# An mLSTM cell and a mixture-of-depths layer on one core: o loads, gates and stores moved back, the expert layers moved from step 8 to step 9

## The chip, the core and the metric

The kernel runs on one core of a Trainium2 chip. Its engines are TensorE (PE, with its weight loads as PEld), VectorE (DVE), ScalarE (ACT), GpSimd (POOL) and SyncE (SP). Each runs its own instructions in order; they wait for one another by semaphores. DMAs are issued by SP (all loads), by ACT (a few at the start) and by POOL (stores, gathers, scatters), and run on the same 16 DMA engines. The metric is the device time of one execution in microseconds (us).

## What is computed

```python
for t in range(S):                       # B, H, S, D = 4, 8, 768, 40
    m_new = maximum(f_gate[t] + m, i_gate[t])
    f_stab, i_stab = exp(f_gate[t] + m - m_new), exp(i_gate[t] - m_new)
    C = f_stab * C + i_stab * outer(v[t], k[t]);  n = f_stab * n + i_stab * k[t]
    y[t] = sigmoid(o_gate[t]) * (C @ q[t]) / maximum(abs(n . q[t]), 1)
# x = y with heads joined: (4, 768, 320); then for each batch b
scores = x @ w_gate
top = the 128 rows of the batch with the largest scores
out = x;  out[top] = x[top] + sigmoid(scores[top]) * (relu(x[top] @ w1) @ w2)     # 320 -> 1024 -> 320
```

All inputs and the output are float32.

## The kernel before, in words

The sequence is cut into 12 steps (N = 12, lines 675 to 742): step n handles 256 positions of batch n // 3, so a batch takes three steps. A step is written out by hand, and what is said of step n mixes the work of several steps:

- `scores(n)` (L291): k times q on PE into pS; `masked(n)` (L303) on DVE multiplies it by the causal mask into P.
- `turn(n + 1, "kT")` (L223): eight PE transposes of the next step's k into two buffers of the pool ps_t, and two ACT copies out of them; `widen(n + 1)` (L214): an ACT copy that spreads q; `turn(n + 1, "qT")`: the same for q, after widen. Where `turn` gets a count, `fill` (L218) first issues that many 128x128 products on constants whose result nobody reads. The counts for steps 0 to 5 are 0, 2, 6, 2, 2 and 4.
- `update(n + 1)` (L259): PE products of k with weighted v into pU; `states(n + 1)` (L271): DVE adds them up to the running states C. pU has one buffer.
- `weigh(n + 2)` (L239): two POOL multiplies of v by the gate factors, into one of three buffers wv.
- `read(n)` (L310) and `attend(n)` (L327): PE products of q with the states, and of P with wv, into pH (one buffer); `divide(n)` (L336): four DVE instructions that give y.
- `sigmoid(n)` (L247): four ACT instructions on the o gate; `output(n)` (L349): two POOL multiplies of y by it into x; `store(n)` (L357): two POOL DMAs of x to the output; `router(n)` (L364): two DVE reductions of x to its scores.

The scores of a batch are ranked when its three steps are done. `spread` (L397) turns the six score columns to rows on PE, ACT copies them, and `ranks` (L425) counts for each row how many scores are larger: three comparisons on DVE (`greater`) and three signs with sums on ACT (`signs`). `select` (L470) makes a one-hot matrix, `numbers` (L513) turns it into row numbers on PE and DVE, `fetch` (L520) gathers the 128 rows of x back from the output on POOL's DMA queue, and `fetched`, `layer1`, `layer2`, `weighed` and `add` run them through the two layers and add the result to the output by an indirect DMA on POOL.

`layers(n)` (L628) holds the two layers of batches 0 and 1, the ranking of batches 1 and 2 and the gates of three steps, in one long stage that takes the place of the rest of step 8. The layers of batch 2 are in the last step and behind it, with those of batch 3.

What sets the order around the change: the program order of each engine, the loads in `queue` (L624), which SP issues at the head of each step, and the rings of four buffers (NB, NO) for k, q, v and o. `load(n)` issues v (2 DMAs), k (2) and q (1), 320 KB each; `load_o(n)` issues the o gate (2 DMAs, 320 KB). A DMA on SP also waits until the one eight places ahead of it has landed. At the start (lines 100 to 107) the order is load 0, load 1, o0, load 2, o1.

Of the kernel before, what the change touches and what calls it, by code (L numbers as in the profile page):

```python
# [26 lines left out]
def _fast(ctx, tc, q, k, v, i_gate, f_gate, o_gate, w_gate, w1_in, w2_in, out):  # L27
# [76 lines left out]
    wg = const.tile([128, DM], FP, name="wg")  # L104
    load_o(0)
    load(2)
    load_o(1)
# [289 lines left out]
    def spread(b, r0, r1, pool=None, copied=True):  # L397

        x, w = x_t[b % 2], r1 - r0
        if pool is None:  # L400
# [6 lines left out]
        return spread_copy(pB, w) if copied else pB  # L407

# [27 lines left out]
    def ranks_third(b, begin):  # L436

        x, d = x_t[b % 2], dep[b]
        if begin:
            d["cnt"] = mod.tile([128, 2 * NS], FP, name="cnt")  # L440
            for r in range(NS):
                greater(b, d["sb"], x[:, r, DM:DM + 1], d["cnt"][:, r:r + 1])
        for r in (NS,) if begin else range(NS + 1, 2 * NS):
            signs(b, d["sb"], x[:, r, DM:DM + 1], d["cnt"][:, r:r + 1])
        if not begin:
            halved(d)
# [173 lines left out]
    def weights2():  # L620
        for h in range(2):
            SP.dma_start(out=w2[:, 4 * h:4 * h + 4], in_=w2_in[512 * h:512 * h + 512].rearrange("(f p) d -> p f d", p=128))

    queue = {0: (load, 3, load_o, 2), 1: (load, 4, load_o, 3, load, 5, load_o, 4), 2: (load, 6, load_o, 5),  # L624
             4: (load, 7, load, 8, weights1, None, load_o, 6), 5: (load_o, 7, weights2, None, load_o, 8), 6: (load, 9),
             7: (load, 10), 9: (load_o, 9, load_o, 10, load, 11, load_o, 11)}

    def layers(n):  # L628
# [9 lines left out]
        sigmoid(n - 2)  # L638
        output(n - 2)
        store(n - 2)  # L640
# [3 lines left out]
        sigmoid(n - 1)  # L644
        output(n - 1)
        store(n - 1)
        layer2(0)
        router(n - 2)
        router(n - 1)
        fetched(1)  # L650
        weighed(0)
        sigmoid(n)
        output(n)
        store(n)
        valued(1)
        layer1(1, 0)
        router(n)
# [7 lines left out]
        dep[2] = {"sb": spread_copy(pB, 2 * NS)}  # L665
        ranks(2)
# [6 lines left out]
        add(1)  # L673

    for n in range(N):
# [7 lines left out]
        if n == 8:  # L683
# [5 lines left out]
        if n in (3, 6, 11):  # L689
            router(n - 1)  # L690
        if n == 4:
            ranks(0)
            select(0)
        if more:
            turn(n + 1, "kT", (0, 2, 6, 2, 2, 4)[n] if n < 6 else 0)
            widen(n + 1)
        if 0 < n and more:
            update(n + 1)
            if n != 9:
                states(n + 1)  # L700
            if n not in (3, 6, 7, 9):
                router(n - 1)
# [5 lines left out]
        if n == 9:  # L708
            numbers(2, ps_s.tile([128, 2, 512], FP, name="pi", tag="s")[:, 0, 0:3])
            states(n + 1)  # L710
        if n + 2 < N and n != 7:
            weigh(n + 2)
        if n == 6:
            fetch(0)
# [3 lines left out]
        if more:  # L718
            turn(n + 1, "qT")
            if n in (3, 7):  # L720
                dep[n // 4] = {"sb": spread(n // 4, 0, 2 * NS)}
# [398 lines left out]
```

## Time and profile before

| | us |
|---|---|
| median of 3 runs (162.68 to 164.01) | 163.51 |
| the profiled execution, device time | 163.37 |
| its span, first to last instruction | 161.3 |
| PE busy (90%) | 144.5 |
| DVE busy | 95.2 |
| ACT busy | 89.0 |
| POOL busy | 84.5 |
| layers stage, from the first scores of step 8 to those of step 9 (78.24 to 108.84) | 30.60 |

The rows of the profile that follow name the line, the engine, the instruction, out<-in, and how many instructions are merged into the row. In a timeline the first column is the start in the span and the second the duration, both in us; in brackets at the end stands how long the engine was idle before it, and what ended that. SPq, ACTq and POOLq are the sequencers, which issue DMAs. Ends of matmuls are modelled, so rows of PE overlap a little.

### The profile page before, as it was taken

The page shows a single profiled execution, that of the slowest core. Times are in us where ns is not written, and L with a number is a line of the kernel's source. Part 1 is how long each engine was busy: PE and PEld are TensorE (multiplying, and loading weights), DVE is VectorE, ACT ScalarE, POOL GpSimd, SP SyncE. Part 2 cuts the span into 40 slices and gives each one's busy share as a digit, 9 for nine tenths or more (in the row PEclk, how much of TensorE's full clock was granted, in tenths as well). Part 3 has the DMA queues.
Part 4 walks back from the last instruction along what each step waited for, and adds up shares of the span by engine and source line. Part 5 has one row for each costly group of instructions (what it writes and reads, how often), then busy time and mean ns, then how long its engine had stood idle before and what let it go on. Part 6 is the DMA issues. An engine that isn't in the chain of part 4 may idle for free.

```text
span 161.3 us, 6676 instructions
## 1 busy us (share of the span) xinstructions
PE 144.5 (90%) x2864; PEld 125.4 (78%) x2864; DVE 95.2 (59%) x251; ACT 89.0 (55%) x179; POOL 84.5 (52%) x114
## 2 busy tenths in 40 slices
PE   7989899998998998899989989799999999999900
PEld 7779789997987987799878779579888897898500
DVE  6478384656769957594596542197776959411000
ACT  1667396566598747425475675874648669213000
POOL 7137278988575492892004969847480924212020
PEclk9999999999999999999999999999999999999995
DMA  4999899999979989999989999999513210330110
GB/s 88 198 163 196 137 169 205 188 186 205 194 169 227 187 161 208 175 262 296 157 240 232 206 266 172 216 190 184 100 45 87 46 39 4 81 41 0 53 51 2
DMA packets 91880, 24.31 MB, mean 151 GB/s; under 512 B 88097, under 2 KB 90466, under 8 KB 91842
## 3 DMA queue, kind: packets, MB, share of 16 engines
q1 hardware_dynamic: 89920, 18.75, 65.1%
q0 software_dynamic: 1728, 4.92, 11.0%
q8 instruction: 24, 0.39, 1.1%
q10 hardware_dynamic: 194, 0.13, 0.3%
q14 instruction: 14, 0.11, 0.2%
HBM read 19.20 MB, written 4.59 MB: 147 GB/s over the span
## 4 chain that ended last, share of the span: by engine, by line
PE 63%; DMA 14%; ACT 7%; issue 5%; DVE 5%; ACTq 1%; POOL 1%; DVEq 0%; POOLq 0%
PE pt L232 10%; DMA k<-in_k_dram 9%; PE pU L267 9%; PE py L576 8%; PE pH L332 7%; PE pH L322 6%; PE pU L560 6%; PE pS L300 4%; PE ph L560 2%; DMA i_sb<-in_i_gate_dram 2%; PE pU L564 2%; DMA xe<-out_dram,idx 2%; PE pX L498 2%; ACT sgn L423 1%; PE pt L221 1%
## 5 line engine op out<-in xcount | busy, mean ns | idle before, releaser
L244 POOL TENSOR_TENSOR wv<-v,cols 64x656 f32<-64x656 f32 x23 | 30.1, 1312 | 25.0 <-DMA v<-in_v_dram 14.1
L354 POOL TENSOR_TENSOR x<-y,so 128x320 f32<-128x320 f32 x24 | 21.1, 896 | 10.9 <-DVE y L346 4.2
L236 ACT COPY qT<-pt 128x512 f32<-128x512 f32 x24 | 13.8, 635 | 17.2 <-PE pt L232 17.2
L250 ACT ACTIVATE so<-o 64x320 f32<-64x320 f32 x48 | 22.4, 467 | 0.9
L234 ACT COPY kT<-pt 128x512 f32<-128x512 f32 x24 | 13.3, 587 | 15.0 <-PE pt L232 15.0
L369 DVE CUSTOM_DVE_ANT_0 scr<-x,wg 128x320 f32<-128x320 f32 x22 | 13.8, 628 | 8.1 <-POOL x L354 6.5
L576 PE MATMUL py<-w,hT 128*128 128x320 f32 x64 | 18.2, 437 | 0.3 <-ACT qT L236 0.3
L279 DVE TENSOR_TENSOR C<-pU,C 128x164 f32<-128x164 f32 x40 | 13.1, 327 | 7.0 <-PE pU L267 5.9
L267 PE MATMUL pU<-wv,k 128*64 128x82 f32 x384 | 16.5, 237 | 0.7 <-issue 0.7
L267 PEld LDWEIGHTS pU<-wv,k 128*64 128x64 f32 x384 | 14.5, 137 | 2.8 <-issue 2.2
L332 PE MATMUL pH<-wv,P 128*64 128x82 f32 x384 | 16.3, 237 | 0.0
L576 PEld LDWEIGHTS py<-w,hT 128*128 128x128 f32 x64 | 11.8, 190 | 5.1 <-ACT qT L236 0.5
L332 PEld LDWEIGHTS pH<-wv,P 128*64 128x64 f32 x384 | 14.4, 136 | 1.8 <-issue 1.0
L232 PE MATMUL pt<-ident,k 128*128 128x128 f32 x96 | 13.7, 279 | 2.3 <-DMA k<-in_k_dram 2.1
L361 POOL DMA_DIRECT2D out_dram<-x x22 | 13.9, 635 | 3.3 <-POOL x L354 3.3
L418 DVE TENSOR_SCALAR_CACHE_REDUCE cmp<-sb,x 128x768 f32<-128x768 f32 (+2 forms) x14 | 12.0, 857 | 6.0 <-ACT sb L412 5.7
L300 PE MATMUL pS<-qT,kT 40*64 40x64 f32 x768 | 14.8, 221 | 0.8 <-issue 0.5
L306 DVE TENSOR_TENSOR P<-pS,mask 128x1024 f32<-128x1024 f32 x12 | 14.6, 1214 | 0.6 <-PE pS L300 0.6
L523 POOL DMA_INDIRECT xe<-out_dram,idx x4 | 4.3, 1086 | 19.9 <-DVE den L341 13.8
L322 PE MATMUL pH<-C,qT 40*64 40x41 f32 x704 | 14.0, 229 | 0.8 <-issue 0.6
L300 PEld LDWEIGHTS pS<-qT,kT 40*64 40x64 f32 x768 | 12.8, 134 | 2.3 <-issue 0.7
L232 PE MATMUL pt<-ident,qw 128*128 128x128 f32 x96 | 13.1, 279 | 1.4 <-ACT qw L216 1.4
(141 smaller groups left out, 229.6 us busy)
## 6 DMA issues: line engine op xcount, KB each, us to landing
k<-in_k_dram SPq DMA_DIRECT2D x24, 160.0 KB, 5.0
q<-in_q_dram SPq DMA_DIRECT2D x12, 320.0 KB, 5.4
v<-in_v_dram SPq DMA_DIRECT2D x24, 160.0 KB, 4.8
o<-in_o_gate_dram SPq DMA_DIRECT2D x24, 160.0 KB, 5.0
out_dram<-x POOLq DMA_DIRECT2D x22, 160.0 KB, 4.4
w<-in_moe_w_dram SPq DMA_DIRECT2D x2, 640.0 KB, 5.8
w<-in_moe_w_dram SPq DMA_DIRECT2D x2, 512.0 KB, 6.0
out_dram<-x SPq DMA_DIRECT2D x2, 160.0 KB, 2.6
```

The lines of the kernel that those rows point to most:

```text
L232: PE.transpose(pt[:, p, :], src[:, c, 2 * p:2 * p + 2, :].rearrange("s j d -> s (j d)"), ident)
L236: ACT.copy(out=T.rearrange("e p (u t) -> e t p u", t=2)[:, c], in_=pt)
L244: (DVE if n == 0 and r else POOL).tensor_tensor(out=wv_t[n % 3][o, :, :, r], in0=v_t[n % NB][o], op=OP.mult, in1=cols[s][o, 0:2, b * H:b * ...
L250: ACT.activation(out=so_t[n % 3][64 * c:64 * c + 64, r], in_=o_t[n % NO][64 * r:64 * r + 64, c], func=AF.Sigmoid)
L267: PE.matmul(pU[64 * j:64 * j + 64, c, p], k_t[n % NB][:, c, 2 * p + j, :], wv_t[n % 3][:, c, 2 * p + j], start=True, stop=True)
L300: PE.matmul(pS[o, j, c, p, :], kT[e, p, t], qT[e, p, t], start=True, stop=True)
L306: DVE.tensor_tensor(out=P.rearrange(flat), in0=pending[n].pop("pS").rearrange(flat), op=OP.mult, in1=mask.unsqueeze(1).to_broadcast([128, ...
L322: PE.matmul(g["pH"][64 * c:64 * c + 64, NP * j + p, r], g["qT"][e, p, t], state[n, 2 * c + r][e, p, :], start=(c, j) not in g["begun"], st ...
L332: PE.matmul(g["pH"][64 * c:64 * c + 64, NP * j + p], g["P"][:, j, c, p, :], wv_t[n % 3][:, c, 2 * p + j], start=(c, j) not in g["begun"], ...
L354: POOL.tensor_tensor(out=x.rearrange(order, j=2, d=D), in0=pending[n]["y"][:, r].rearrange("s (j p) d -> s j p d", j=2), in1=o.rearrange(o ...
L361: (POOL if n < N - 1 else SP).dma_start(out=out[b, a:a + 128, :].rearrange("(r t) d -> t r d", t=64), in_=x_t[b % 2][64 * c:64 * c + 64, 2 ...
L576: PE.matmul(d["py"], hT_t[:, f, half(b)], w2[:, f, :], start=(f == 0), stop=(f == NF - 1))
```

## The change

1. Loads: at the start load 2 is issued ahead of o0, and o1 moves to step 0. In `queue` each o load moves behind one or more k, q, v loads; load 9 goes from step 6 to step 5, ahead of the weights of the first layer; load 10 stays in step 7, ahead of o8; load 11 goes from step 9 to step 8.
2. Gates: the sigmoids of step n move to a later step (`gated_at`), the multiplies to x too (`made`), and the router (`scored`). Steps 1, 5 and 8 have no sigmoid.
3. Stores: those of steps 0 to 2 are issued together in step 4, those of steps 3 to 5 at the end of step 7.
4. `layers` is called in step 9. The sigmoids, output and store of step 9 are now inside it, behind the copy of batch 2's scores. `add(1)` moves out of it to step 10, where it follows `fetch(2)`; `fetch(2)` itself now stands before the q transposes of step 10, it stood at the end of step 9.
5. No fillers: `turn` is called without a count.
6. Ranking of batch 0: its spread is in step 4 in two halves (four and two columns) through the transposes' pool ps_t (`spread_halves`), with two ACT copies; the comparisons are in steps 5 and 6, the three signs in step 5, the selection and the numbers in step 6, the gather in step 7, there ahead of `weigh(9)`. The spread of batch 1 is in step 8.

```diff
     load(1)
     wg = const.tile([128, DM], FP, name="wg")
+    load(2)
     load_o(0)
-    load(2)
-    load_o(1)
...
+    def spread_halves(b):
+        x = x_t[b % 2]
+        sb = mod.tile([128, 128 * 2 * NS], FP, name=f"sb{2 * NS}", bufs=1)
+        for r0 in (0, 4):
+            w = min(4, 2 * NS - r0)
+            pB = ps_t.tile([128, w, 128], FP, name="pB", tag="t")
+            for r in range(w):
+                PE.transpose(pB[:, r, :], x[:, r0 + r, DM:DM + 1].to_broadcast([128, 128]), ident)
+            ACT.copy(out=sb[:, 128 * r0:128 * (r0 + w)], in_=pB.rearrange("p r t -> p (r t)"))
+        return sb
...
+    def compare(b, r0, r1):
+        x, d = x_t[b % 2], dep[b]
+        if r0 == 0:
             d["cnt"] = mod.tile([128, 2 * NS], FP, name="cnt")
+        for r in range(r0, r1):
+            (greater if r < NS else signs)(b, d["sb"], x[:, r, DM:DM + 1], d["cnt"][:, r:r + 1])
...
-    queue = {0: (load, 3, load_o, 2), 1: (load, 4, load_o, 3, load, 5, load_o, 4), 2: (load, 6, load_o, 5),
-             4: (load, 7, load, 8, weights1, None, load_o, 6), 5: (load_o, 7, weights2, None, load_o, 8), 6: (load, 9),
-             7: (load, 10), 9: (load_o, 9, load_o, 10, load, 11, load_o, 11)}
+    queue = {0: (load, 3, load_o, 1), 1: (load, 4, load_o, 2, load, 5), 2: (load, 6, load_o, 3), 3: (load, 7),
+             4: (load, 8, load_o, 4), 5: (load, 9, load_o, 5, weights1, None, load_o, 6), 6: (weights2, None, load_o, 7),
+             7: (load, 10, load_o, 8), 8: (load_o, 9, load, 11), 10: (load_o, 10, load_o, 11)}
+    gated_at = {0: 0, 2: 1, 3: 2, 4: 3, 6: 4, 7: 5, 10: 10}
+    made = {0: 0, 2: 1, 3: 2, 5: 3, 6: 4, 7: 5, 10: 10}
+    scored = {1: 0, 3: 1, 4: 2, 6: 3, 7: 4, 8: 5, 10: 9}
...
         turn(n + 1, "qT")
         dep[2] = {"sb": spread_copy(pB, 2 * NS)}
+        sigmoid(9)
+        output(9)
+        store(9)
         ranks(2)
...
-        add(1)
...
-        if n == 8:
+        if n == 9:
             layers(n)
...
+        if n == 5:
+            compare(0, 0, 2)
+        if n == 6:
+            compare(0, 2, 3)
+            halved(dep[0])
             select(0)
         if more:
-            turn(n + 1, "kT", (0, 2, 6, 2, 2, 4)[n] if n < 6 else 0)
+            turn(n + 1, "kT")
             widen(n + 1)
+        if n == 5:
+            compare(0, 3, 4)
...
+        if n == 10:
             numbers(2, ps_s.tile([128, 2, 512], FP, name="pi", tag="s")[:, 0, 0:3])
             states(n + 1)
+            fetch(2)
+            add(1)
+        if n == 7:
+            fetch(0)
+        if n < 8:
             weigh(n + 2)
+        if n == 4:
+            for i in range(3):
+                store(i)
...
             turn(n + 1, "qT")
+            if n == 5:
+                compare(0, 4, 6)
+            if n in gated_at:
+                sigmoid(gated_at[n])
+            if n == 6:
+                numbers(0, spare(n + 1)[:, 1, 0:3])
...
         attend(n)
+        if n in (4, 8):
+            dep[n // 8] = {"sb": spread_halves(n // 8)}
         divide(n)
+        if n in made:
+            output(made[n])
+            if n > 8:
+                store(n)
+        if n == 7:
+            for i in range(3, 6):
+                store(i)
```

More of the change, by code (lines that the diff above doesn't have):

```diff
@@ L637, in layers @@
         fetch(1)
[L638 to L640 removed]
+        sigmoid(6)
+        output(6)
+        store(6)
         layer1(0, 4)
```

55 lines of the change are left out of this document (16 added, 39 removed).

## The prediction

> **What bounds the kernel now.** I read the page's first line and the windows of the steps, then PE's timeline for the clean length of a step and its holes, then SP's timeline for the order in which loads are issued, then ACT, DVE and POOL where the change inserts something. First the span, and the stretch of steps 1 to 7 (from the first scores of step 1 to those of step 8; behind the busy times stand PE's granted clock, the DMA engines' share and GB/s):
>
> ```profile
> span 161.3 us, 6676 instructions
> ```
> ```profile
> 20.96:78.24 57.28, 54.54 (x1476) 48.64 (x1474) 38.90 (x100) 36.60 (x68) 38.60 (x55) 1.00 0.98 203
> ```
> ```profile
> 22.26 0.33 PE L300 MATMUL pS<-qT,kT 40*64 40x64 f32 x3 [0.16 <-issue]
> ...
> 65.58 0.63 PE L232 MATMUL pt<-ident,k 128*128 128x128 f32 x4 [0.44 <-DMA k<-in_k_dram]
> ...
> 70.80 1.16 PE L300 MATMUL pS<-qT,kT 40*64 40x64 f32 x64
> 71.89 1.09 PE L232 MATMUL pt<-ident,k 128*128 128x128 f32 x8
> 72.92 1.35 PE L267 MATMUL pU<-wv,k 128*64 128x82 f32 x32
> ...
> 75.28 1.09 PE L232 MATMUL pt<-ident,qw 128*128 128x128 f32 x8
> 76.20 0.82 PE L405 MATMUL pB<-ident,x 128*128 128x128 f32 x6
> 76.95 1.36 PE L332 MATMUL pH<-wv,P 128*64 128x82 f32 x32
> 78.24 1.16 PE L300 MATMUL pS<-qT,kT 40*64 40x64 f32 x64
> ...
> 88.63 4.57 PE L576 MATMUL py<-w,hT 128*128 128x320 f32 x16
> ...
> 115.76 1.15 PE L300 MATMUL pS<-qT,kT 40*64 40x64 f32 x60
> ...
> 123.16 1.16 PE L300 MATMUL pS<-qT,kT 40*64 40x64 f32 x64
> ...
> 127.73 0.32 PE L405 MATMUL pB<-ident,x 128*128 128x128 f32 x1 [0.32 <-DVE x L369]
> ```
> ```profile
> L221 PE MATMUL pt<-hot 128*128 128x128 f32 x32 | 4.9, 291 | 0.0
> ```
>
> PE and the DMA engines are both full in steps 1 to 7: PE is busy for 54.54 of 57.28 us, and the DMA share is 0.98. Step 7 runs without a hole: 78.24 - 70.80 = 7.44 us, of which the spread of one batch's scores is 0.66, so a clean step is 6.78. Inside it kT starts at +1.09, update at +2.12, qT at +4.48, and 2.30 remain from qT to the end. Seven clean steps, two spreads and the numbers of one batch (0.3) are 49.1 us; steps 1 to 7 take 57.28. The 8.2 us between are the fillers (4.9) and holes, most of them waits for k. But the fillers stand just ahead of the k transposes: where k is late, taking them out leaves a wait of the same length. So the gain depends on when loads land.
>
> **The loads.** With engines this full, a load moves by what leaves or enters SP's queue ahead of it.
>
> ```profile
> 10.93 2.48 SPq L75 DMA_DIRECT2D o<-in_o_gate_dram  x2
> ...
> 18.11 1.39 SPq L69 DMA_DIRECT2D q<-in_q_dram  x1
> ...
> 37.23 2.37 SPq L75 DMA_DIRECT2D o<-in_o_gate_dram  x2
> ...
> 41.62 2.33 SPq L65 DMA_DIRECT2D k<-in_k_dram  x2
> ...
> 46.56 1.68 SPq L75 DMA_DIRECT2D o<-in_o_gate_dram  x2
> ...
> 50.12 2.87 SPq L65 DMA_DIRECT2D k<-in_k_dram  x2
> ...
> 54.66 2.44 SPq L75 DMA_DIRECT2D o<-in_o_gate_dram  x2
> ...
> 58.88 3.47 SPq L65 DMA_DIRECT2D k<-in_k_dram  x2
> ...
> 68.59 2.35 SPq L615 DMA_DIRECT2D w<-in_moe_w_dram  x1
> ```
> ```profile
> q0 software_dynamic: 1728, 4.92, 11.0%
> ...
> o<-in_o_gate_dram SPq DMA_DIRECT2D x24, 160.0 KB, 5.0
> ```
>
> An o load holds the queue 2.1 us (mean of 2.37, 1.68 and 2.44). A pair of stores goes out on POOL's queue, but on the same engines: q0's 4.92 MB take 11.0% of 161.3 = 17.7 us, so 0.33 MB take 1.2. Ends: 0, if stores fit into gaps, and 2.1, an o load's price for the same bytes; I take 1.2, which is measured on that queue. A load's second half is issued about 1.2 us behind its first (half of 2.4) and lands 5.0 later.
>
> k first. Load 5 now has one o load and two pairs fewer ahead: 41.62 - 2.37 - 2.4 = 36.9, landed by 43.1. Load 6 has two and three pairs fewer: 50.12 - 4.05 - 3.6 = 42.5, landed by 49.7. Load 7: 58.88 - 4.05 - 1.2 = 53.6 (four pairs go, three return in step 4), landed by 59.9. All three are on time for the steps below, so PE's waits for k go.
>
> Now o, which is moved back. o0 goes behind load 2: 18.11 + 1.39 - 2.48 = 17.0, landed 23.2. o3 was ahead of load 5 and is now behind load 6, where o5 was, less o3, o4 and four pairs: 54.66 - 4.05 - 4.8 = 45.8, landed 52.0. o4 follows load 8, where the weights were, less two o loads and two pairs: 68.59 - 4.1 - 2.4 = 62.1, landed 68.3. o5 follows o4 and a load (37.23 + 2.37 to 46.56 is 6.96, less a pair 5.8): 70.0, landed 76.2.
>
> **The change, part by part.** The gates' sigmoids stay in ACT's in-order queue behind the qT copies, and what follows them there waits when o is late: the kT copies and the widening of q, for which PE's qT waits, and in step 4 the two copies of the spread scores, which free both buffers that the k transposes need.
>
> ```profile
> 23.78 1.07 ACT L234 COPY kT<-pt 128x512 f32<-128x512 f32 x2
> 24.88 0.72 ACT L216 COPY qw<-q 128x640 f32<-128x640 f32 x1
> ...
> 45.20 1.95 ACT L250 ACTIVATE so<-o 64x320 f32<-64x320 f32 x4
> ...
> 99.37 0.60 ACT L566 ACTIVATE hT<-ph 128x512 f32<-128x512 f32 x1 [1.90 <-PE ph L564]
> ```
>
> Of POOL I need the multiplies, the gather of batch 2 with what stands behind it, the add of batch 1, and how long a gather takes to land:
>
> ```profile
> 108.98 1.90 POOL L589 DMA_INDIRECT out_dram<-yg,idx  x1 [0.59 <-POOL wv L244]
> ...
> 116.42 1.09 POOL L523 DMA_INDIRECT xe<-out_dram,idx  x1 [0.27 <-DVE den L341]
> 117.93 1.69 POOL L354 TENSOR_TENSOR x<-y,so 128x320 f32<-128x320 f32 x2 [0.42 <-DVE y L346]
> ```
> ```profile
> DMA to landing us min/median/max: 3.1/3.2/6.6
> ```
> ```profile
> L244 POOL TENSOR_TENSOR wv<-v,cols 64x656 f32<-64x656 f32 x23 | 30.1, 1312 | 25.0 <-DMA v<-in_v_dram 14.1 <-DVE cols L206 6.0 <-DMA out_dram<-yg,idx 4.2
> ```
>
> - Step 1: scores end at 22.26 + 0.33 = 22.6 as now, qT could start at 26.0. o0 lands at 23.2, three of four sigmoids (0.49 each) remain, then 1.07 and 0.72: 26.5. Cost 0.5. Steps 2 and 3 are clean: they end at 35.6 and 42.4.
> - Step 4: clean to 49.2, spread to 49.8, scores of step 5 to 50.9. o3 lands at 52.0; three sigmoids to 53.5, the first copy of the spread (0.5, the size of a kT copy) to 54.0. Only then may k be transposed. **Cost 3.1**, the largest new wait.
> - Step 7: o4 at 68.3, three sigmoids, 1.07 and 0.72 end at 71.6; qT's slot is 71.2 (step 5 ends 59.7, step 6 66.7). Cost 0.35.
> - Step 8: the first gather is now issued ahead of weigh(9), whose second half waits for its landing. Output(4) on POOL ends near 71.2, behind o4's gates (69.8) and two multiplies, the first begun before them. From issue to landing 3.2 (median) to 6.6 (longest); I take the middle, 4.9, as the queue is full there. With 1.3 for the second half: 77.4 against an update slot of 75.9. Cost 1.5 (ends 0 and 3.2). The wait for o5's gates (0.9) lies within it.
>
> - Stores later: six at once in steps 4 and 7, on a POOL that waits for v there anyway; their DMA time is in the sums above. No cost beside.
> - Ranking in steps 4 to 7: the same instructions, six transposes and two copies instead of one. Three signs go to step 5, which has no gate, so ACT has room: nothing. It also takes away step 4's wait for q behind three signs, counted in the 8.2.
> - Weights come with o5 ahead of them and load 9: w2's second half lands near 90 by the same count and is asked for at 88.63 + 4.5 = 93.1, as the layers now start at 82.7 (step 7 ends 73.8; 6.78, 0.66 and 1.5 follow). Nothing. o8 lands near 101, one to two us behind its slot in the layers; ACT is idle for 1.90 right behind it (99.37), so I take 0.3 (ends 0 and 2.5).
> - Layers in step 9: the same work, but the gates of step 9 now stand between the copy of batch 2's scores and its three signs.
>
> ```profile
> 107.19 0.19 ACT L423 ACTIVATION_READ_ACCUMULATOR sgn<-sb,x 128x1 f32 x1
> 108.44 0.96 DVE L472 TENSOR_TENSOR sel<-iota,cnt 128x768 bf16<-128x768 f32 x1
> 109.67 1.05 DVE L279 TENSOR_TENSOR C<-pU,C 128x164 f32<-128x164 f32 x3
> 110.95 1.35 PE L267 MATMUL pU<-wv,k 128*64 128x82 f32 x32
> ```
>
> The signs end at 107.4, then the selection (109.4), then the states, which release pU at 110.7; PE writes pU at 110.95. There is 0.2 of slack. 1.95 more on ACT delays this chain: cost 1.8.
>
> - Step 10: add(1) is put behind the gather of batch 2 on POOL and must wait for its landing, as both touch the output. Behind it stands output(10), then the last scores, then the spread for which PE waits already (127.73).
>
> The gather can go about 2 us earlier than now, lands 3.2 later, and 1.9 follow: 5.1 from its issue, where 1.5 lie between gather and output now. 5.1 - 2.0 - 1.5 = 1.6 late, less the 0.3 that PE waits already: cost 1.3 (ends 0 and 3.3).
>
> **The sum.** From 8.2 I take off the hole of 0.5 in step 1's scores, which stays: -7.7. A plain step 8 (6.78) takes the place of step 10 (123.16 - 115.76 = 7.40): -0.6. Costs: 0.5 + 3.1 + 0.35 + 1.5 + 0.3 + 1.8 + 1.3 = 8.9. Span 161.3 - 8.3 + 8.9 = 161.9. The profiled execution took 163.37, so 2.1 lie around the span: 164.0, against its own 163.37 and the median of 163.51.
>
> **Rivals.**
> Faster: the queue drains quicker and o3 is there when ACT asks. If stores cost 2.1 a pair, o3 lands 3.6 earlier, at 48.4, and the 3.1 of step 4 go; with the later gates on time too, 0.9 more: 164.0 - 4.0 = 160.0. It decides from a landing by 48.9. For it: queues held by buffer releases are gone. Against: k4 to k6 now come at a steady pace under a share of 0.98.
>
> Slower: PE stands idle for 3.1 us before step 5's k. The granted clock is 1.00 in every stretch quoted, but the longest hole there is under 0.7. If the clock halves behind a hole of this length, the rest of that step (5.7) doubles at worst: 164.0 + 5.7; I take half, 166.9. It decides where the hole outlasts the clock's patience. [...]
>
> Slower as well: the gather lands at 6.6 and POOL's chain in step 10 costs its upper end: 164.0 + 1.7 + 2.0 = 167.7.
>
> No effect: PE already hides everything, so that only waits change names. That is nearly the forecast; it says 163.4.
>
> **How the numbers follow.** Forecast, with the second no-effect case, 0.50, by itself 162 to 166; faster rival, whole or in part, 0.29; the two slower ones 0.21. The range reaches to 160.0 and to 168.0. 1% (1.6 us) is about what can be told from no change. Above 165.1 lie the slower rivals and a third of the forecast: 0.38; below 161.9 the faster one: 0.30; between 0.32.
>
> **What would show it.** Right: no waits for k in steps 2 to 6; ACT's gates of step 4 waiting for o until about 52; PE idle about 3 us ahead of the k transposes of step 5; layers starting near 82.7; PE's update in step 10 waiting for DVE; add(1) waiting for the gather. Wrong: o3 landed before 49, a granted clock under 1.00 in steps 5 or 6, or a wait for weights.

## The result, and the profile after

The changed kernel takes 175.86 us (median of 4 runs, 174.80 to 176.88) where the kernel before takes 163.76 (4 runs on the same chip, 162.68 to 164.12): ratio 1.075, 95% interval 1.067 to 1.083. It is slower, by more than the range forecast. The profiled execution took 176.88 us with a span of 175.0. Single executions of one kernel differ by some us, the longer ones mostly at a lower mean clock (beside experiment 4 the kernel before took 163.34 at 0.987 and 173.22 at 0.954), and the ratios compare undisturbed executions alone.

Windows by stage, first one of before, then four of after (from, to and length; then the busy times of PE, PEld, DVE, ACT and POOL; PE's granted clock; DMA share; GB/s):

```profile
123.16:161.30 38.14, 29.42 (x347) 24.92 (x344) 15.09 (x44) 13.62 (x36) 10.34 (x11) 0.95 0.15 34
```
```profile
51.41:64.33 12.92, 8.84 (x210) 7.88 (x209) 5.99 (x12) 7.19 (x14) 7.51 (x10) 0.74 1.06 219
...
88.47:123.74 35.27, 31.15 (x339) 25.58 (x338) 16.49 (x40) 21.87 (x48) 18.15 (x21) 0.90 0.89 178
123.74:132.09 8.35, 7.00 (x217) 6.32 (x214) 6.67 (x19) 4.06 (x10) 3.82 (x3) 1.00 0.14 31
132.09:175.00 42.91, 31.03 (x347) 26.23 (x344) 13.62 (x44) 13.62 (x36) 12.79 (x13) 0.90 0.18 38
```

With the other windows of both kernels that gives this table (us). The forecast's column is its own timetable: step 5 begins at 50.9 - 1.1, ends at 59.7, the layers begin at 82.7, and step 10 is the old step 9 (6.92) with the cost of 1.8 (rounded, the column adds up to 161.7, its sum is 161.9).

| stage | before | after | difference | forecast |
|---|---|---|---|---|
| up to the scores of step 5 | 54.51 | 51.41 | -3.1 | 49.8 |
| step 5 | 8.19 | 12.92 | +4.7 | 9.9 |
| the other plain steps up to 10 (before 6, 7, 9, 10; after 6, 7, 8, 10) | 29.86 | 32.49 | +2.6 | 31.7 |
| layers | 30.60 | 35.27 | +4.7 | 30.9 |
| last stage, from the scores of step 11 | 38.14 | 42.91 | +4.8 | 39.4 |

The gain came: before step 5 the kernel is 3.1 us ahead, and no step waits for k any more (in the page of after the group of the k transposes, L231, is idle for 4.1 us in all, and ACT ends all of it). Then the other four rows give back 16.8. PE's timeline shows most of it, each wait in brackets:

```profile
56.65 1.97 PE L231 MATMUL pt<-ident,k 128*128 128x128 f32 x8 [4.08 <-ACT sb L419]
58.55 2.46 PE L266 MATMUL pU<-wv,k 128*64 128x82 f32 x32
```
```profile
92.22 0.58 PE L299 MATMUL pS<-qT,kT 40*64 40x64 f32 x9 [2.70 <-issue]
...
93.56 1.93 PE L321 MATMUL pH<-C,qT 40*64 40x41 f32 x48
95.42 2.45 PE L331 MATMUL pH<-wv,P 128*64 128x82 f32 x32
```
```profile
127.28 1.35 PE L266 MATMUL pU<-wv,k 128*64 128x82 f32 x32 [1.35 <-DVE C L278]
...
139.63 0.48 PE L406 MATMUL pB<-ident,x 128*128 128x128 f32 x1 [3.41 <-DVE x L368]
...
140.54 3.09 PE L569 MATMUL pU<-xeT,w 128*128 128x128 f32 x16
```

Waits are only half of it. Behind the long ones the same rows take up to twice as long: the eight transposes 1.97 (1.09 elsewhere), the update 2.46 (1.35), attend 2.45 (1.36), layer 1 3.09. The clock itself shows why. These are windows of after of 3.41 us each, set on the times at which the granted clock changes:

```profile
50.75:54.17 3.42, 1.82 (x70) 1.36 (x67) 2.92 (x7) 0.47 (x1) 3.42 (x6) 1.00 1.02 220
54.17:57.58 3.41, 0.93 (x5) 0.93 (x6) 0.67 (x1) 2.26 (x5) 0.31 (x1) 0.50 1.06 286
57.58:60.99 3.41, 3.41 (x41) 2.90 (x39) 1.37 (x4) 2.83 (x5) 1.93 (x2) 0.50 0.89 180
60.99:64.33 3.34, 3.34 (x107) 3.03 (x105) 1.64 (x5) 1.63 (x3) 2.50 (x3) 1.00 1.26 183
```
```profile
91.71:95.13 3.42, 2.91 (x58) 2.41 (x60) 2.26 (x4) 1.42 (x4) 0.00 (x0) 0.50 0.76 154
95.13:98.54 3.41, 3.41 (x43) 3.15 (x40) 2.76 (x6) 2.45 (x6) 0.00 (x0) 0.50 1.06 162
```
```profile
139.50:142.91 3.41, 3.11 (x14) 2.82 (x15) 1.61 (x6) 0.59 (x1) 3.29 (x4) 0.50 0.42 96
```

In this trace the granted clock is either 1.00 or 0.50, and the times at which it changes lie whole multiples of 3.41 us apart: it falls at 54.17, 91.71 and 139.50 (11 and 14 times 3.41 apart), for two, two and one windows, and then not before PE's last product. In the window ahead of the first fall PE stood for 1.60 us (3.42 - 1.82); in the next, at half clock, for 2.48, and the one behind that was at half too. PE was busy for 4.34, 6.32 and 3.11 us at half clock in these three places (0.93 + 3.41, 2.91 + 3.41, 3.11); half of that, 6.9 us in all, is an estimate of what a whole clock would have saved (the slow rows less their lengths elsewhere give 6.2).

What made PE wait shows on the other engines. ACT in step 4, then POOL in steps 10 and 11:

```profile
52.77 0.47 ACT L249 ACTIVATE so<-o 64x320 f32<-64x320 f32 x1 [2.75 <-DMA o<-in_o_gate_dram]
54.54 1.45 ACT L249 ACTIVATE so<-o 64x320 f32<-64x320 f32 x3 [1.30 <-DMA o<-in_o_gate_dram]
56.01 0.86 ACT L419 COPY sb<-pB 128x512 f32<-128x512 f32 x2
```
```profile
131.41 1.11 POOL L532 DMA_INDIRECT xe<-out_dram,idx  x1 [4.46 <-PE pt L231]
135.82 1.66 POOL L598 DMA_INDIRECT out_dram<-yg,idx  x1 [3.30 <-ACT so L249]
137.55 1.67 POOL L353 TENSOR_TENSOR x<-y,so 128x320 f32<-128x320 f32 x2
```

ACT's gates of step 4 wait for both halves of o3; the copies of the spread scores come last and PE's transposes wait for them. On POOL the add waits from 132.5 until behind the landing of the gather (135.02 by the trace; the name in the bracket, ACT, had long been done), and output(10) starts at 137.55.

The hole of 2.70 (a stretch in which PE stands) is put down to "issue": PE waited for nothing that a semaphore shows. The trace has 24 packets of 16 KB of kind instruction (queue q8, 0.39 MB), and each of the seven holes of PE over 0.2 us that are put down to issue in the steps ends 1.4 to 1.8 us behind the end of such a packet, here at 90.75. These holes also stand 256 PE instructions or a multiple of that apart (with 449, 705, 1473, 3265, 3521, 3777 and 4033 of them ahead; in before the three holes stand at 449, 3777 and 4801). From that comes the estimate that a packet brings 256 instructions (the trace has 5742 of PE's, 239 for each of the 24), and that PE had run out of them. Call each such place in PE's instructions a mark. The packet that ended the long hole took 0.96 us, as others do, but it started late: 5.0 us behind PE's passing of the mark before (84.78), where the four packets ahead of it started 1.6 to 2.1 us behind theirs. The 16 DMA engines, of whose time these packets take 1.0% over the span, also carried this:

```profile
w<-in_moe_w_dram SPq DMA_DIRECT2D x2, 640.0 KB, 9.1
```

The two halves of weights 2 took 8.6 and 9.5 us from issue to landing, against 5 for a load of k, q or v, and the half of an o load issued right behind them 9.3; six stores went out beside them (81.6 to 85.2).

### The profile page after: what moved, and what is told of

It reads as the page before. It is cut to its first block, busy times and chain, and to the rows that moved or that the text cites. A ratio compares the mean times of both kernels' runs of the same rounds, so it can differ in the third digit from the quotient of the medians.

```text
span 175.0 us, 6617 instructions
## 1 busy us (share of the span) xinstructions
PE 148.0 (85%) x2832; PEld 128.4 (73%) x2832; DVE 95.4 (55%) x251; ACT 88.9 (51%) x181; POOL 85.6 (49%) x114
## 4 chain that ended last, share of the span: by engine, by line
PE 48%; SPq 11%; issue 10%; DMA 9%; ACT 9%; DVE 5%; POOL 3%; POOLq 0%; DVEq 0%; ACTq 0%
PE pt L231 8%; SPq L65 7%; PE pH L331 7%; PE pU L569 6%; DMA o<-in_o_gate_dram 6%; PE py L585 5%; PE pU L266 4%; PE pH L321 4%; PE pS L299 4%; DMA xe<-out_dram,idx 4%; PE ph L569 2%; ACT so L249 2%; PE pU L573 2%; ACT kT L233 2%; SPq L75 2%
## 5 line engine op out<-in xcount | busy, mean ns | idle before, releaser
L243 POOL TENSOR_TENSOR wv<-v,cols 64x656 f32<-64x656 f32 x23 | 31.3, 1363 | 24.8 <-DMA v<-in_v_dram 11.8
L266 PE MATMUL pU<-wv,k 128*64 128x82 f32 x384 | 17.9, 247 | 2.1 <-DVE C L278 1.3
L299 PE MATMUL pS<-qT,kT 40*64 40x64 f32 x768 | 15.3, 223 | 4.9 <-issue 4.6
L266 PEld LDWEIGHTS pU<-wv,k 128*64 128x64 f32 x384 | 15.6, 144 | 4.6 <-issue 3.0
L331 PE MATMUL pH<-wv,P 128*64 128x82 f32 x384 | 17.4, 246 | 0.0
L231 PE MATMUL pt<-ident,k 128*128 128x128 f32 x96 | 13.9, 291 | 4.1 <-ACT sb L419 4.1
L278 DVE TENSOR_TENSOR C<-pU,C 128x164 f32<-128x164 f32 x40 | 13.1, 328 | 7.2 <-PE pU L266 6.1
L331 PEld LDWEIGHTS pH<-wv,P 128*64 128x64 f32 x384 | 15.4, 144 | 1.7 <-issue 1.2
L321 PE MATMUL pH<-C,qT 40*64 40x41 f32 x704 | 14.8, 235 | 0.5 <-issue 0.5
L321 PEld LDWEIGHTS pH<-C,qT 40*64 40x64 f32 x704 | 13.3, 140 | 2.2 <-issue 1.3
L231 PEld LDWEIGHTS pt<-ident,k 128*128 128x128 f32 x96 | 11.1, 148 | 5.0 <-ACT sb L419 4.2
```

What stands on the lines that cost most here:

```text
L231: PE.transpose(pt[:, p, :], src[:, c, 2 * p:2 * p + 2, :].rearrange("s j d -> s (j d)"), ident)
L243: (DVE if n == 0 and r else POOL).tensor_tensor(out=wv_t[n % 3][o, :, :, r], in0=v_t[n % NB][o], op=OP.mult, in1=cols[s][o, 0:2, b * H:b * ...
L266: PE.matmul(pU[64 * j:64 * j + 64, c, p], k_t[n % NB][:, c, 2 * p + j, :], wv_t[n % 3][:, c, 2 * p + j], start=True, stop=True)
L299: PE.matmul(pS[o, j, c, p, :], kT[e, p, t], qT[e, p, t], start=True, stop=True)
L321: PE.matmul(g["pH"][64 * c:64 * c + 64, NP * j + p, r], g["qT"][e, p, t], state[n, 2 * c + r][e, p, :], start=(c, j) not in g["begun"], st ...
L331: PE.matmul(g["pH"][64 * c:64 * c + 64, NP * j + p], g["P"][:, j, c, p, :], wv_t[n % 3][:, c, 2 * p + j], start=(c, j) not in g["begun"], ...
```

## The experiments

The theory: four waits (o3 late; PE's instructions late behind weights 2 and the stores; the add behind the gather; gates ahead of the signs). The first three cost PE over 1.6 us each, with half clock behind, the fourth 1.35 at whole clock. The main rival: the slow rows come from something else, such as the missing fillers. In the edits `...` stands for lines left out, and of `queue` only the entries that change are shown.

**1. o3 ahead of load 6.**

```diff
-2: (load, 6, load_o, 3)
+2: (load_o, 3, load, 6)
```

> The changed kernel (175.9) with o3 issued ahead of load 6 instead of behind it. Theory (o3 lands too late, the gates of step 4 block ACT ahead of the copies of the spread scores, and the wait of 4.08 also drops the clock): o3 is issued some 10 us earlier, PE's wait before the k transposes of step 5 falls from 4.08 to under 0.5, kT returns from 1.97 to 1.09 and the update of that step from 2.46 to 1.35, step 5 takes about 7.0 instead of 12.92: some 5.6 us, so about 170.3. Rival 1 (the load is only exchanged for another: k of step 6 or 7 comes late by the 2.1 us of an o load): the wait moves to step 6 or 7 and the time is 172 to 174. Rival 2 (the rows of step 5 are slow for want of the fillers, not for the wait): the wait goes, the slow rows stay: about 172.3.

Measured: 170.14 (169.5 to 170.8), 1.035 times before (1.027 to 1.044); after stands at 1.075.

```profile
51.66:59.43 7.77, 7.30 (x210) 6.31 (x209) 5.34 (x11) 5.62 (x11) 7.57 (x10) 1.00 1.01 204
59.43:68.82 9.39, 7.38 (x200) 6.57 (x198) 7.37 (x15) 4.29 (x9) 4.94 (x5) 1.00 0.88 195
68.82:79.35 10.53, 8.72 (x212) 7.71 (x209) 6.13 (x20) 5.33 (x10) 4.75 (x5) 0.84 1.06 194
...
87.39:117.28 29.89, 28.18 (x339) 23.03 (x339) 16.82 (x40) 21.86 (x48) 18.10 (x21) 1.00 1.04 224
```

Step 5 falls from 12.92 to 7.77 at whole clock: the wait and the slow rows went together. The total is as expected (5.7), but not by this alone. The layers fell by 5.4, because the instructions came in time there (no hole, though weights 2 still took 8.6 us to land, 9.1 in after), and steps 6 and 7 grew by 1.7 and 3.2: a new hole of 1.75 for instructions behind the six stores, and, as the steps now come earlier, the same wait for the next gate (o4, PE idle for 1.77, with a half clock behind it: 0.84 over step 7).

**2. Fillers in two waits of the changed kernel.**

```diff
         if n == 5:
+            fill(spare(n + 1)[:, 0, :], 13)
             compare(0, 0, 2)
...
             fetched(b - 1, 2)
+            fill(ps_t.tile([128, 128], FP, name="pf", tag="t"), 10)
```

> The changed kernel with 13 filler products ahead of the k transposes of step 5 (13 x 0.29 = 3.8 us in a wait of 4.08) and 10 ahead of the spread of step 11 (2.9 us in a wait of 3.41). Nothing is ready earlier by it. Theory (an idle PE of 3 to 4 us loses granted clock, and the rows behind run slow): the waits are filled, the rows behind return to 1.09 (kT of step 6), 1.35 (update) and 1.95 (layer 1 in the last stage, now 3.09); 2.0 and 1.1 to 1.4 us less, so 172.5 to 172.9. Rival (the slow rows come from the DMA load or the kind of work there, or the stages are bound by another engine): rows stay slow, or are fast with no gain, time 175.9; if the fillers outlast the waits, up to 176.5.

Measured: 169.38 (166.7 to 171.8; too far apart for an interval), the profiled one 166.67.

```profile
51.77 3.17 PE L220 MATMUL pU<-hot 128*128 128x128 f32 x26
54.77 1.04 PE L231 MATMUL pt<-ident,k 128*128 128x128 f32 x8
55.74 1.35 PE L266 MATMUL pU<-wv,k 128*64 128x82 f32 x32
...
130.44 0.32 PE L406 MATMUL pB<-ident,x 128*128 128x128 f32 x1 [0.69 <-DVE x L368]
...
131.25 1.95 PE L569 MATMUL pU<-xeT,w 128*128 128x128 f32 x16
```

(Each product is two records.) Products that compute nothing make the kernel faster: transposes 1.04, update 1.35, layer 1 1.95, all at whole clock, step 5 9.73 and the last stage 41.50. These rows are the clock by itself, 2.0 us in step 5 and 1.5 in the last stage. The other 1.2 us of step 5 are not: o3 landed at 52.41 in this execution (54.52 in after), so the wait was shorter too. Nor are the further 3.7 us in the layers (31.56) the edit's: a hole of 1.77 for instructions came there too, but lay across two of the windows of 3.41 us, 0.49 and 1.28 us, and the clock stayed at 1.00. That such holes fall differently from run to run fits the spread, but only one of the four runs has a trace.

**3. Stores 3 to 5 spread over steps 5 to 7.**

```diff
             output(made[n])
-            if n > 8:
-                store(n)
-        if n == 7:
-            for i in range(3, 6):
-                store(i)
+            if made[n] > 2:
+                store(made[n])
```

> The changed kernel with the stores of steps 3, 4 and 5 right behind their outputs (in steps 5, 6 and 7) instead of all six at the end of step 7. Theory (six stores and the two halves of weights 2 crowd the DMA engines between 82 and 92 us, PE's next 16 KB of instructions come late, PE stands for 2.70 inside the scores of step 9 and loses clock): the landing times of the halves fall from 8.6 and 9.5 towards 6, the hole falls under 1.0, layer 1 and the rows before it return to full clock, layers 35.3 to about 31 us: about 171.4. Rival (the hole comes from the place in PE's code or from weights 2 alone): a hole of 2 us or more stays, time 175.9. Second rival: the stores taken earlier delay loads 9 and o5 and give back up to 1.2 a pair: 173.

Measured: 175.76 (174.3 to 177.9), 1.060 (1.048 to 1.073). A miss: weights 2 land in 6.9, but PE still waits 1.88 at the same place (PE row below), and the clock falls behind it (0.95 over the layers). The hole is not made by these stores alone; it is 0.8 shorter in this execution.

```profile
90.65 0.38 PE L299 MATMUL pS<-qT,kT 40*64 40x64 f32 x9 [1.88 <-issue]
```

**4. Weights 2 behind load 10 and o8.**

```diff
-6: (weights2, None, load_o, 7), 7: (load, 10, load_o, 8),
+6: (load_o, 7), 7: (load, 10, load_o, 8, weights2, None),
```

> The changed kernel with the two halves of weights 2 behind load 10 and o8 in SP's queue, some 6 us later, so that they are issued in the layers' stage, where PE uses few instructions per us. The stores stay bunched. Theory (each half is 0.66 MB that SP hands over faster than the engines move it; the queues get 8 to 9 us deep in step 8, a plain step that uses up instructions quickly, and PE's next 16 KB come late): the hole of 2.70 in the scores of step 9 falls under 0.6, the half clock behind it (6.8 us, of which 6.3 busy) goes; 2.2 + 3.1 less, so about 170.5. Rival 1 (the hole belongs to its place in PE's code or to the stores): it stays near 2, time 175 to 176. Rival 2 (weights 2 then lands too late for layer 2 of batch 0): the hole goes and PE waits there for w2 by 1 to 2 us: 172 to 173.

Measured: 174.33 (173.8 to 176.0), 1.063 (1.051 to 1.076).

```profile
92.89:122.78 29.89, 28.18 (x339) 23.03 (x338) 16.82 (x40) 21.86 (x48) 18.10 (x21) 1.00 0.84 181
```
```profile
53.41:56.82 3.41, 0.00 (x0) 0.00 (x0) 0.78 (x1) 1.97 (x5) 1.40 (x3) 1.00 1.05 273
56.82:60.23 3.41, 2.87 (x22) 2.54 (x24) 2.04 (x4) 2.19 (x5) 1.41 (x2) 0.50 1.03 207
60.23:63.65 3.42, 3.42 (x87) 3.17 (x86) 1.64 (x5) 1.41 (x3) 2.85 (x3) 0.50 1.11 190
63.65:67.06 3.41, 3.41 (x32) 3.08 (x34) 0.00 (x0) 2.15 (x4) 0.00 (x0) 0.50 0.90 169
```

The hole of the layers is gone, and they take 29.89 instead of 35.27: the expected 5.3. Two other places took most of it back in this execution. In step 8, where other loads now stand, a hole of 1.63 came. And the wait of step 5, untouched by the edit and 4.47 long here, filled one window of 3.41 us whole; the clock then stayed at half for three windows, the last two of them fully busy, and step 5 took 15.75.

**5. The add of batch 1 back at the end of the layers.**

```diff
     def layers(n):
...
         states(n + 1)
+        add(1)
...
             fetch(2)
-            add(1)
```

> The changed kernel with the add of batch 1 back at the end of the layers' stage. Theory (the add behind the gather of batch 2 waits for its landing and holds output(10), and the 3.41 that PE then waits in step 11 also costs clock): PE's wait ahead of the spread in step 11 falls from 3.41 to about 0.3, layer 1 behind it from 3.09 to about 1.95; 3.1 + 1.2 less: about 171.5. Rival 1 (the clock there is not tied to the wait): only the wait goes, 172.8. Rival 2 (the gather of batch 2 then stands behind the add and lands as late, so another engine ends as late): over 174.5.

Measured: 171.13 (164.75, 170.5, 171.8 and 172.2), the profile taken at 172.23.

```profile
132.35:170.50 38.15, 29.50 (x346) 24.92 (x344) 13.55 (x44) 13.61 (x36) 11.82 (x12) 0.96 0.17 38
```
```profile
136.90 0.32 PE L406 MATMUL pB<-ident,x 128*128 128x128 f32 x1 [0.22 <-DVE x L368]
137.06 1.95 PE L569 MATMUL pU<-xeT,w 128*128 128x128 f32 x16
```

The last stage is back at before's 38.14; the edit is worth 4.76 there (3.4 of wait, 1.1 in layer 1). The total fits the 171.5 expected as far as runs this far apart can tell; the profiled execution is 4.65 under that of after.

**6. The gates of step 9 behind the signs of batch 2.**

```diff
-        sigmoid(9)
-        output(9)
-        store(9)
         ranks(2)
+        sigmoid(9)
+        output(9)
+        store(9)
```

> The changed kernel with the gates, output and store of step 9 behind the signs of batch 2. Theory (the gates hold the signs, the signs hold the selection, the selection holds the states that free pU): the wait of 1.35 ahead of the update in step 10 falls to about 0.1; step 10 takes 7.0 instead of 8.35. The time of one run can not tell 1.35. Rival (output(9) comes later by it and delays something behind it on POOL): the wait goes, the last stage grows by as much.

Measured: one run, 179.4. DVE in after, then DVE, PE and POOL here:

```profile
124.12 0.69 DVE L446 TENSOR_SCALAR cnt<-cnt 128x3 f32<-128x3 f32 x1 [1.86 <-ACT sgn L436]
```
```profile
122.35 0.17 DVE L446 TENSOR_SCALAR cnt<-cnt 128x3 f32<-128x3 f32 x1
```
```profile
129.56 2.45 PE L266 MATMUL pU<-wv,k 128*64 128x82 f32 x32 [3.59 <-POOL wv L243]
```
```profile
123.26 1.83 POOL L353 TENSOR_TENSOR x<-y,so 128x320 f32<-128x320 f32 x2 [4.14 <-ACT so L249]
...
126.68 2.83 POOL L243 TENSOR_TENSOR wv<-v,cols 64x656 f32<-64x656 f32 x2
```

DVE's wait for the signs went (1.86 before), which shows the mechanism. But output(9) now waits for its gates on POOL ahead of the weighing of step 11, and PE's update waits 3.59 for that, more than twice what was mended, with half clock behind it. Step 10 takes 14.49 at a mean clock of 0.68. The rival had the engine right and the place wrong.

**7. The kernel before without its fillers.**

```diff
-            turn(n + 1, "kT", (0, 2, 6, 2, 2, 4)[n] if n < 6 else 0)
+            turn(n + 1, "kT")
```

> The kernel before, with its 16 filler products of steps 0 to 5 taken out and nothing else. Theory (the fillers fill waits for k; taken out without the moved loads, most of their 4.9 us turn into waits of the same length, each under the 1.6 us of idle in a window of 3.4 us that cost clock so far): span within 2 us of before, 161.5 to 164, granted clock as before. Rival 1 (the fillers hold the clock up): a half clock of 3.4 us or more in steps 3 to 6, 165 to 168. Rival 2 (the fillers are pure cost): 4 to 5 us less, about 159.

Measured: 168.25 (165.1 to 170.9), 1.009 (0.991 to 1.028), no difference that can be told.

```profile
20.92:77.78 56.86, 51.18 (x1444) 45.08 (x1442) 41.86 (x101) 36.69 (x68) 38.64 (x55) 1.00 1.00 206
81.47:84.88 3.41, 1.72 (x38) 1.46 (x34) 3.09 (x8) 2.95 (x6) 0.00 (x0) 1.00 0.95 319
84.88:88.30 3.42, 3.42 (x18) 3.20 (x17) 0.80 (x1) 0.00 (x0) 0.00 (x0) 0.50 1.08 203
```

Steps 1 to 7 take 56.86, with the fillers 57.28. PE is busy for 3.4 us less (51.18 instead of 54.54), and 2.9 of that has become idle time (5.7 now, 2.7 before; the holes now are 1.77, 0.61 and 0.28 for k, 1.23 for q's widening, 1.48 for DVE), at whole clock. So the fillers neither cost nor hold up anything in the steps: the rival that their absence slows the rows fails. The span is 164.3 because of a hole for instructions, now in the layers: PE idle for 1.69 of one window, half clock in the next.

**8. All four places mended, first version.** The edits of 1, 4, 5 and 6 together, and o4 ahead of load 8.

```diff
-4: (load, 8, load_o, 4),
+4: (load_o, 4, load, 8),
```

> The changed kernel with five places mended: o3 ahead of load 6 and o4 ahead of load 8, weights 2 behind o8, the add of batch 1 back at the end of the layers, the gates of step 9 behind the signs of batch 2. Theory (the costs are those waits and the clock lost behind them, and they add up): steps 5 to 7 about 7.7 each, layers about 30, step 10 about 7.0, the last stage 38.1 as before: span 158, time about 160, under the kernel before. Rival (each mended wait uncovers the next of its size, for k of step 8 or for weights 2): 163 to 167.

Measured: 176.29 (173.8 to 178.6), 1.069 (1.051 to 1.086), a clear miss.

```profile
102.26 2.47 PE L585 MATMUL py<-w,hT 128*128 128x320 f32 x4 [7.03 <-DMA w<-in_moe_w_dram]
```

Steps 5 to 7 came near the 7.7 forecast (7.88, 8.85, 7.93). But the layers now begin 3 us earlier than in the changed kernel and 7 earlier than in 4, and weights 2, moved back, are too late for them (7.03, and three windows of half clock, 0.50 from 97.25 to 107.49), and the weighing of step 11 waits as in 6 (3.60). Mends that work alone need not add up.

**9. Second version.** As 8, but weights 2 where the change has them, the weighing of step 9 ahead of the first gather, that of step 11 ahead of output(9).

```diff
         sigmoid(9)
-        output(9)
-        store(9)
         layer2(1)
...
         weigh(n + 2)
+        output(9)
+        store(9)
...
-        if n == 7:
-            fetch(0)
         if n < 8:
             weigh(n + 2)
+        if n == 7:
+            fetch(0)
```

> The changed kernel with o3 ahead of load 6, o4 ahead of load 8, the add of batch 1 back at the end of the layers, the gates of step 9 behind the signs of batch 2 and the weigh of step 11 ahead of output(9), the weigh of step 9 ahead of the first gather; weights 2 where the change has them. Theory (the costs are single waits with the half clock behind them; the two that the last version uncovered, on weights 2 and on the weigh of step 11, were made by its own moves): steps 5 to 7 take 7.9, 8.8 and 7.9 as there, step 8 about 8.2, layers 29.9, step 10 about 7.0, the last stage 38.1: span 159, time about 161, 1.5% under the kernel before. Rival 1 (another hole of over 1.6 us in one window appears, in step 8 or in the layers, for PE's instructions or for weights 2, with 3.4 to 6.8 us at half clock behind it): 164 to 167. Rival 2 (what each mend gains, the next queue gives back): 170 and more.

Measured: 168.27 (167.4 to 170.9), 1.029 (1.015 to 1.042).

```profile
61.04 0.57 PE L299 MATMUL pS<-qT,kT 40*64 40x64 f32 x21 [1.48 <-issue]
...
77.59 0.93 PE L299 MATMUL pS<-qT,kT 40*64 40x64 f32 x48 [1.38 <-issue]
```

Rival 1: layers 29.89 and step 10 6.93 as hoped, but two holes for instructions, in steps 6 and 8, each with about one window of half clock (mean clock 0.83 and 0.84), make them 10.25 and 10.74. And as output(9) now stood ahead of the add of batch 1, the gather waited for the add; the last stage was 43.2.

**10. Third version.** As 9, and the stores one pair a step, the add ahead of output(9), router(9) behind the numbers of batch 2.

```diff
-    scored = {1: 0, 3: 1, 4: 2, 6: 3, 7: 4, 8: 5, 10: 9}
+    scored = {1: 0, 3: 1, 4: 2, 6: 3, 7: 4, 8: 5}
...
+        add(1)
         output(9)
...
         states(n + 1)
-        add(1)
...
             states(n + 1)
+            router(9)
             fetch(2)
...
-        if n == 4:
-            for i in range(3):
-                store(i)
...
-        if n == 7:
-            for i in range(3, 6):
-                store(i)
+        if 3 <= n <= 8:
+            store(n - 3)
```

> The last version with three more places mended: the stores of steps 0 to 5 one pair a step (3 to 8) instead of two groups of six; the add of batch 1 ahead of output(9); router(9) behind the numbers of batch 2 and ahead of the gather, so that the gather is issued near where the kernel before has it. Theory (six stores at once hold up PE's next 16 KB of instructions, 1.48 and 1.38 us in steps 6 and 8, each with 3.4 us at half clock behind; in step 11 the gather waited 4.79 for an add that stood behind output(9)): steps 6 and 8 take about 7.3 each instead of 10.25 and 10.73, the last stage 38.1 instead of 43.2: span 155 to 156, time about 157.5, 4% under the kernel before. Rival 1 (the late instructions come from the sum of the DMA load, not from the stores being bunched): one of the two holes stays, with its half clock: 161 to 163, the kernel before's time. Rival 2 (stores in steps 3 to 8 delay k of steps 6 to 8 by 1.2 a pair): waits for k of 1 to 2 us, 160 to 164.

Measured: 162.61 (12 runs, 161.0 to 164.7) beside 163.15, ratio 0.997 (0.993 to 1.001): the kernel before's time, which is rival 1's figure, and not the 157.5 of the theory. The granted clock is 1.00 in each stage from step 5 to step 10, and 0.93 in the last (0.95 in before).

```profile
54.25 0.63 PE L231 MATMUL pt<-ident,k 128*128 128x128 f32 x4 [1.55 <-DMA k<-in_k_dram]
...
76.50 0.93 PE L299 MATMUL pS<-qT,kT 40*64 40x64 f32 x48 [1.11 <-issue]
```

The hole of step 6 is gone and the last stage takes 38.5; a wait for k in step 5 and 1.11 and 0.74 of late instructions in step 8 are left. Rivals 1 and 2 hold in part each.

**11. The same with the stores in two groups again.**

```diff
+        if n == 4:
+            for i in range(3):
+                store(i)
...
-        if 3 <= n <= 8:
-            store(n - 3)
+        if n == 7:
+            for i in range(3, 6):
+                store(i)
```

> The last version with one thing put back: the stores of steps 0 to 5 in two groups of six, as the change has them. Theory (six stores at once hold up PE's next instructions in steps 6 and 8): holes of 1.2 us or more, put down to issue, come back in the scores of steps 6 and 8 (1.48 and 1.38 in the version before), with a half clock of 3.4 us behind at least one; the wait for k of 1.55 in step 5 goes; together +1.5 to +4 us, 164 to 166.6. Rival (which hole comes is a matter of the moment, and the stores have no part in it): 161 to 163, holes like those of the last version (1.11 and 0.74 in step 8, none in step 6).

Measured: 164.62 (164.3 to 166.1), 1.010 (1.002 to 1.019).

```profile
60.55 0.57 PE L299 MATMUL pS<-qT,kT 40*64 40x64 f32 x21 [1.21 <-issue]
...
81.88 1.97 PE L231 MATMUL pt<-ident,qw 128*128 128x128 f32 x8 [2.62 <-ACT qw L215]
```

The hole of step 6 is back and the wait for k gone: six stores at once do hold up PE's instructions there (holes of 1.75, 1.20, 1.48 and 1.21 in the versions of 1, 8, 9 and 11, none in the two with spread stores). In step 8 no hole for instructions came; instead ACT waited for o5, the widening of q stood behind the gates, and PE waited 2.62 with half clock behind (0.74 over the step). So the theory holds for step 6 and not for step 8.

**12. The third version with the stores a step later.**

```diff
-        if 3 <= n <= 8:
-            store(n - 3)
+        if 4 <= n <= 8:
+            store(n - 4)
+        if n == 8:
+            store(5)
```

> The last version with the spread stores one step later (step 4 to 8, two pairs in step 8), so that two pairs fewer stand ahead of k of step 6. Theory (the 1.55 that PE waits for k in step 5 are one to two pairs of stores at 1.2 us each): that wait falls to 0.5 or less, nothing else changes: about 161.5, 1% under the kernel before. Rival (the second pair in step 8 makes the holes there, 1.11 and 0.74 now, larger, past the idle time that costs the clock): 163 to 165.

Measured: 163.92 (12 runs, 161.6 to 165.9) beside 163.64, ratio 0.998 (0.993 to 1.003). Step 5 takes 6.96, without the wait for k, but PE waits 1.11 for k in step 7 and 2.65 in step 8 for the same gate (o5) as in 11, and the time is that of 10. No version beats the kernel before by more than can be measured.

## Why the prediction was wrong

The mechanisms were mostly right, their order of size was not, and two terms were missing. The gap of 13.1 us of span (175.0 against 161.9), step by step:

- **The loads: right.** No wait for k is left in steps 2 to 6. The gain came out 1.6 smaller by step 5 (51.41 against 49.8), 0.4 in step 1, 0.85 in step 3 (a hole for instructions of 0.65 in it) and 0.35 in step 4, which the clean step did not allow for.
- **Step 4, "cost 3.1, the largest new wait": right in cause, near in size.** o3 landed at 54.52 instead of 52.0, the wait was 4.08. The faster rival, which needed it by 48.9, fell with that.
- **The slower rival, the clock: it was the case, and in three places instead of one.** The prediction put 2.9 on step 5 and made it hang on the length of one hole. Measured by the estimate above: 2.2 in step 5, 3.2 in the layers, 1.6 in step 11, 6.9 in all (6.2 by the rows), about half of the gap. This is the main step that failed: the sum put the clock at nothing, and no run shows that a hole of 3.1 us is free of it, or that the length of one hole decides. What the runs show is idle time by window of 3.41 us. Whole-clock windows followed by half clock had 1.60, 2.20 and 3.28 us of it in after, 1.69 in experiment 7 and all 3.41 in experiment 4. Those with the most that were followed by whole clock had 1.53 and 1.10 in before and 1.35 in after. A hole of 1.77 that two windows shared (0.49 and 1.28, experiment 2) cost no clock.

  A count of work fits these two traces better than idle time: the window of after from 91.71, at half clock itself, had only 0.50 us of idle and was followed by half clock. The count is an estimate from the rows. Each product record counts its columns times the rows and columns that its row names, as a share of 128*128 (one of the scores, `40*64 40x64`, counts 64 x 40/128 x 64/128 = 10; a transpose 128), shared out where it lies across the end of a window. The traces of before (from 4.25 us on) and after (from 6.38) have 91 windows up to PE's last product. The five followed by half clock count 70, 463, 686, 740 and 1183, the 86 followed by whole clock 1523 and more. The count was made up on these same traces, and no run tests it.
- **Layers: forecast +0.3, measured +4.7.** The hole of 2.70 and 2.8 us of slow rows behind it are more than that; without them the stage takes 29.89 (experiments 1 and 4). This is the second step that failed: PE's instructions were not a term at all. The change puts weights 2 into step 8, which is now a plain step; before it was the layers. A plain step has some 210 products and as many weight loads in 6.8 us, the layers 339 in 30; by these counts 256 instructions last about 4 us in a plain step and 11 in the layers (an estimate), and the packet ended 6.0 us behind the mark before. Moving weights 2 alone removes the hole (experiment 4). That the packet is held up by them on the DMA engines is the author's estimate, which the times fit (it starts 5.0 us behind the mark before, the four ahead of it 1.6 to 2.1); the trace does not show when it was asked for, and no run tells whether it stood behind all of weights 2 or shared the engines with them.
- **Step 10, sigmoid(9) ahead of the signs: right,** 1.35 for 1.8. **The add behind the gather: right in kind, at its upper end,** 3.3 for 1.3, the third step, a term of the right kind that was sized too small. Against the scores next to it the gather went 1.3 us earlier, not 2 (0.66 behind those of step 10 before, 0.68 ahead of those of step 11 now), and the add took until 6.1 us behind its issue to let output(10) start (5.1 forecast). The wait then lost the clock as well (0.50 from 139.50 to 142.91).
- **Not there:** 0.35 for o4 and 1.5 for the first gather. Both were hidden by the lateness of step 5; with that mended (experiment 1) the wait for o4 came, at 1.77.
- **Two slips in the working, without effect on the sum:** by its own numbers load 6 lands at 48.7 and not 49.7, and the fillers were 3.4 us of PE's time in the steps (experiment 7) and not 4.9.

Besides, the terms do not add. Each mend made the steps earlier and uncovered the next late load, and three waits counted for more than their length: by the estimate above those of 4.08, 2.70 and 3.41 us lost another 2.2, 3.2 and 1.6 by the clock. With all places mended the changed kernel stands where the kernel before stood, at 0.997: it is 3.7 us ahead by step 5 (50.78 against 54.51 in experiment 10), and the later steps give that back.

## What to carry to other kernels

Cost a wait of PE by the window as well as by its length: here 1.60, 2.20 and 3.28 us of idle within a window of 3.41 brought two, two and one windows at half clock on top, and in experiment 2 two waits filled with products on constants gave back 2.0 and 1.5 us of slow rows. Instructions were DMA packets too (24 of 16 KB), and a late one stopped PE for 2.70 us: keep bursts of large DMAs out of stretches in which PE uses many small products, and read "issue" holes against the instruction packets. Before moving work later in an in-order queue, list what stands behind it on that engine; experiments 6, 8 and 9 each made a larger wait by skipping that.

## What was not expected of the hardware

- The return of the clock was not set by PE's busy time alone. The windows at half clock that PE filled from 57.58 and from 95.13 in after were followed by whole clock, that from 60.23 in experiment 4 (3.42 us busy) by half, and in the last stage of after a window with 3.11 us busy was followed by whole. The count of work above tells them apart: 1876, 1636 and 1622 in after, and about 1270 in experiment 4 (an estimate from its rows: 19 of the update's products at 41, the 64 reads at 6.4, half a transpose at 128). The reads, `40*64 40x41`, took 1.95 us there (1.14 at whole clock) and add only 410 to the count.
- PE's instructions come as packets among the DMA's: 24 of 16 KB in before and in after (queue q8, 0.39 MB), and the holes put down to issue end 1.4 to 1.8 us behind the end of one (seven holes in after, three in before).
- Two DMAs of 640 KB in after, issued 1.5 us apart, took 8.6 and 9.5 us to land where the loads of 160 to 320 KB took 4.7 to 5.3 in the median, and 160 KB issued right behind them took 9.3.
